# The guard in a float64 weight decode: from ScalarE and VectorE to VectorE and GpSimd

## The chip, the core and the metric

The kernel runs on one NeuronCore of a Trainium2 chip. The core has five engines that each take their own instructions strictly in order: TensorE (PE, with its weight loads shown apart as PEld), VectorE (DVE), ScalarE (ACT), GpSimd (POOL) and SyncE (SP), which here only issues DMAs. The metric is the device time of one execution in microseconds, lower is better. Before the change three runs gave 763.26, 766.6 and 768.91 us, with a median of 766.6 us.

## The reference, cut to what matters

Attention over hash buckets, followed by a gated feed-forward with a short convolution, for 4 batches of 768 rows and 8 heads of 64:

```
q_bucket, k_bucket = 6 sign bits of q @ proj, k @ proj
scores = 0.125 * q @ k.T, masked to -1e9 where the buckets differ
attn   = exp(scores - max) / (sum + 1e-9);  x = attn @ v, heads side by side
h      = relu(x @ w_in)                       # 512 -> 1024
conv   = 3-tap convolution of h along the sequence, weights conv_w
out    = (h * sigmoid(conv)) @ w_out          # 1024 -> 512
```

The inputs `w_in`, `conv_w` and `w_out` are float64. The chip computes in 32 bits, so the kernel reads each weight as two 32-bit words and rebuilds it as a sum of two float32 parts before TensorE uses it. That decode is where the change lies.

## The kernel before, in words

**Attention.** The 32 heads are handled as 16 pairs, and each pair in 12 units of 128 query rows for one head, 192 units in all. A unit multiplies queries with keys into PSUM (`products`, line 250), VectorE copies the scores to SBUF and takes their row maximum (`maximum`, line 260, with a small scaling at line 262), ScalarE takes the exponential (line 265), TensorE transposes the result (line 280), ScalarE copies that back (line 287), and after each four units TensorE multiplies with the values (line 306, 24 matmuls in a row, preceded by two transposes at line 301). VectorE scales that result (`x`, line 315) and GpSimd splits it (lines 316 and 317). VectorE also forms the reciprocal sums (lines 270 and 271) that GpSimd spreads into `rec` (line 274). So four units make one round, about 10 to 11 us long in this part of the program.

**The next pair.** While one pair runs, GpSimd splits the next pair's queries and keys, in tile `R`, into two parts (`hi` at line 168, the rest at line 173), VectorE takes the hash bits (line 186) from a TensorE product (line 183), and SyncE copies the parts to their places (lines 171, 175 and 192). Only when all that has read `R` can the following pair be loaded into it (line 155).

**The weights.** There are 16 blocks of 128 rows by 512 columns, 8 of `w_in` (tiles `wui`, `wli`, `rawi`) and 8 of `w_out` (`wuo`, `wlo`, `rawo`), and one small block of 24 columns for the convolution. One block is decoded per round, from about 30 us to about 212 us in the profile. A block passes through these instructions: the absolute value of the high word on ScalarE (line 86); on VectorE the compare-and-multiply that zeroes small weights (line 88), the shift (line 90), the merge (line 92), the mask (line 94) and the low product (line 96); on ScalarE the rounding (line 104); on GpSimd a subtraction (line 106) and an addition (line 108).

**The order.** All order is written out by hand. The decode is a Python generator, and `background` (line 128) moves every open block one step on per unit: it runs a generator until it yields a number that is at least `stop`, which is 1 during the attention units. So `yield 0` keeps two instructions in the same unit, and `yield 1` or `yield 2` puts the next instruction into the next unit. Blocks that were opened earlier are moved on first. Each engine then executes what stands in its own queue from first to last.

Of the kernel before, what the change touches and what calls it, by code (L numbers as in the profile page):

```python
# [9 lines left out]
I32 = mybir.dt.int32  # L10
U32 = mybir.dt.uint32
AF = mybir.ActivationFunctionType
ALU = mybir.AluOpType
# [12 lines left out]
SCALE = 0.125  # L26
BIG = float(2 ** 33)
MASKED = -8.0e9
F64_MIN = 2.0 ** -15 * 1.125
LAG, EB = 3, 5  # L30
DEFER = 2
FLAG = 3
# [10 lines left out]
def lsh_attention_conv_ffn(ctx, tc, qk, v, hw, w_in, conv_w, w_out, consts, ident_in, out):  # L43
    nc = tc.nc
# [7 lines left out]
    def ring(pool, bufs, shape, dtype, tag, name):  # L52

        k = turns[tag] = (turns.get(tag, -1) + 1) % bufs
        return pool.tile(shape, dtype, tag=f"{tag}{k}", name=name, bufs=1)
# [17 lines left out]
    def decode(raw, n, name):  # L73

        pr = raw.rearrange("p (n two) -> p n two", two=2)  # L80
        lo, hi = pr[:, :, 0].bitcast(U32), pr[:, :, 1].bitcast(F32)
        up, low = (ring(wp, bufs, [P, WC], I32, f"w{x}", f"w{x}{name}")[:, :n]
                   for x, bufs in (("u", 3), ("l", 3)))
        upf, lowf = up.bitcast(F32), low.bitcast(F32)
        V = nc.vector
        nc.scalar.activation(lowf, hi, AF.Abs)
        yield 2
        V.scalar_tensor_tensor(upf, lowf, F64_MIN, hi, ALU.is_ge, ALU.mult)
        yield 1
        V.tensor_scalar(low, up, 3, 0x3FFFFFFF, ALU.logical_shift_left, ALU.bitwise_and)  # L90
        yield 0
        V.scalar_tensor_tensor(up, up, -0x40000000, low, ALU.bitwise_and, ALU.bitwise_or)  # L92
        yield 2
        V.tensor_scalar(low, up, -0x800000, None, ALU.bitwise_and)
        yield 0
        V.scalar_tensor_tensor(lowf, lo, 2.0 ** -52, lowf, ALU.mult, ALU.mult)  # L96
        return upf, lowf

    def split_weight(raw, name):

        up, low = yield from decode(raw, WC, name)
        yield 2
        blk = weights[name] = cp.tile([P, 2, WC], F32R, tag=f"w{name}", name=f"w{name}")
        nc.scalar.copy(blk[:, 0, :], up)
        yield 2
        nc.gpsimd.tensor_tensor(up, up, blk[:, 0, :].bitcast(F32), ALU.subtract)
        yield 1
        nc.gpsimd.tensor_tensor(blk[:, 1, :], up, low, ALU.add)

    def decode_taps(raw):  # L110
        up, low = yield from decode(raw, NFC * 3, "cw")
        nc.vector.tensor_tensor(cw.rearrange("p f k -> p (f k)"), up, low, ALU.add)
# [419 lines left out]
```

## Time and profile before

| | |
|---|---|
| median of 3 runs | 766.6 us (763.26 to 768.91) |
| the profiled execution | 764.44 us, of which its span is 761.6 us |
| PE busy | 722.1 us, 95% of the span |
| ACT busy | 511.9 us, 67% |
| DVE busy | 486.1 us, 64% |
| POOL busy | 294.9 us, 39% |
| mean granted TensorE clock | 0.992 of full speed |

Busy time says how long an engine was executing, not whether anything waited for it. What sets the end is read from the chain of waits, which follows each instruction back to whatever released it. [...] The 2.84 us between the span and the execution's time lie outside the instructions.

### The profile page before, as it was taken

Reading aid. Unit: us, or ns where it says so; the run is one execution under the profiler, and the core shown is the slowest. Engines: PE = TensorE matmul, PEld = TensorE weight load, DVE = VectorE, ACT = ScalarE, POOL = GpSimd, SP = SyncE. Lnnn points to the kernel's source line nnn. Section 1 sums busy time; section 2 is a strip of 40 time slices with the busy share of each in tenths; the row PEclk is TensorE's granted clock in tenths of the full one; section 3 lists DMA queues with packets and bytes.
Section 4 is the critical chain, followed back from the end, with each engine's and each line's share of the span. In section 5 each row is a group of like instructions: output and inputs, shape, how many; then the busy total and the mean of one; then the engine's idle time right before and its main releaser. Section 6 shows DMA issues by size and latency. Waiting matters only on the chain.

```text
span 761.6 us, 12950 instructions
## 1 busy us (share of the span) xinstructions
PE 722.1 (95%) x4648; PEld 595.3 (78%) x4648; DVE 486.1 (64%) x1032; ACT 511.9 (67%) x954; POOL 294.9 (39%) x325
## 2 busy tenths in 40 slices
PE   5989989888889999999999999999999999999997
PEld 3867767665679987777889988777778998778986
DVE  7789978777857555555546655555546665554663
ACT  5877768777755558777765557777775556775554
POOL 4355765566536221433424421333424421113222
PEclk8999999999999999999999999999999999999999
DMA  4666576484422111445632202256361211000011
GB/s 138 157 181 191 128 195 165 117 230 108 116 50 65 60 42 64 118 123 150 140 105 53 73 1 105 48 147 154 95 174 40 63 42 62 2 1 1 0 43 41
DMA packets 30351, 72.13 MB, mean 95 GB/s; under 512 B 5936, under 2 KB 7504, under 8 KB 30288
## 3 DMA queue, kind: packets, MB, share of 16 engines
q1 hardware_dynamic: 30000, 71.27, 34.7%
q8 instruction: 36, 0.59, 0.3%
q14 instruction: 27, 0.22, 0.1%
q10 hardware_dynamic: 288, 0.05, 0.0%
HBM read 27.40 MB, written 6.29 MB: 44 GB/s over the span
## 4 chain that ended last, share of the span: by engine, by line
PE 69%; DVE 18%; DMA 5%; ACT 3%; issue 2%; POOL 1%; SPq 1%; DVEq 0%; POOLq 0%; ACTq 0%
PE o L365 18%; PE h L335 17%; PE v L306 14%; PE t L280 10%; DVE e L260 9%; PE s L250 9%; DMA R<-in_qk 2%; ACT at L287 2%; DMA k<-R 2%; DVE x L315 1%; PE hash L183 1%; PE v L301 1%; DVE wuo L92 1%; DVE wlo L96 1%; DVE st L262 1%
## 5 line engine op out<-in xcount | busy, mean ns | idle before, releaser
L260 DVE TENSOR_SCALAR_CACHE_REDUCE e<-s 128x768 f32<-128x768 f32 x192 | 182.9, 953 | 108.2 <-PE s L250 100.4
L265 ACT ACTIVATE e<-e,st 128x768 f32<-128x768 f32 x192 | 180.8, 941 | 30.0 <-DVE st L262 22.2
L287 ACT COPY at<-t 128x768 f32<-128x768 f32 x192 | 151.8, 792 | 61.1 <-PE t L280 61.1
L280 PE MATMUL t<-ident,e 128*128 128x128 f32 x1152 | 161.5, 277 | 17.4 <-DVE e L260 15.2
L280 PEld LDWEIGHTS t<-ident,e 128*128 128x128 f32 x1152 | 133.0, 141 | 40.1 <-DVE e L260 33.5
L344 DVE SCALAR_TENSOR_TENSOR ht<-ht,cw 128x384 f32<-128x384 f32 (+1 forms) x128 | 113.9, 890 | 71.1 <-ACT ht L342 67.4
L365 PE MATMUL o<-wo,g 128*128 128x512 f32 x576 | 143.0, 394 | 1.0 <-POOL g L354 1.0
L335 PE MATMUL h<-xh,wi 128*128 128x386 f32 x512 | 142.2, 341 | 1.0 <-ACT ht L340 1.0
L306 PE MATMUL v<-at,v 128*64 128x256 f32 x1152 | 137.0, 383 | 0.0
L354 POOL TENSOR_TENSOR g<-ht,g 128x384 fp32r<-128x384 f32 x64 | 72.0, 1124 | 151.9 <-ACT g L353 120.1
L365 PEld LDWEIGHTS o<-wo,g 128*128 128x128 f32 x576 | 107.3, 188 | 21.9 <-POOL g L354 1.4
L250 PE MATMUL s<-K,Q 128*128 128x384 f32 x384 | 117.5, 387 | 3.7 <-DVE e L260 2.7
L274 POOL TENSOR_SCALAR rec<-sums 128x256 f32<-128x256 f32 x48 | 19.5, 406 | 246.7 <-ACT at L287 146.7
L306 PEld LDWEIGHTS v<-at,v 128*64 128x64 f32 x1152 | 82.0, 137 | 41.2 <-issue 7.9
L250 PE MATMUL s<-k,q 96*128 96x384 f32 x384 | 99.8, 341 | 2.3 <-DVE e L260 2.2
L335 PEld LDWEIGHTS h<-xh,wi 128*128 128x128 f32 x512 | 94.1, 188 | 5.0 <-ACT ht L340 1.5
L347 ACT ACTIVATE ht<-ht 128x384 f32<-128x384 f32 x64 | 33.6, 526 | 90.4 <-DVE ht L344 90.2
L335 PE MATMUL h<-xl,wi 128*128 128x386 f32 x256 | 86.8, 339 | 0.0
L250 PEld LDWEIGHTS s<-K,Q 128*128 128x128 f32 x384 | 58.9, 192 | 34.5 <-issue 19.0
L250 PEld LDWEIGHTS s<-k,q 96*128 96x128 f32 x384 | 71.1, 192 | 3.1 <-ACT q L230 3.1
L348 DVE TENSOR_TENSOR ht<-ht 128x384 f32<-128x384 f32 x64 | 43.4, 679 | 33.7 <-ACT ht L347 33.4
L173 POOL TENSOR_TENSOR R<-R,hi 128x768 fp32r<-128x768 f32 x30 | 58.9, 1964 | 0.7
(70 smaller groups left out, 632.9 us busy)
## 6 DMA issues: line engine op xcount, KB each, us to landing
R<-in_qk SPq DMA_DIRECT2D x15, 768.0 KB
K<-hi SPq DMA_DIRECT2D x60, 192.0 KB
v<-in_v SPq DMA_DIRECT2D x16, 384.0 KB
out<-osb SPq DMA_DIRECT2D x24, 256.0 KB
Q<-hi SPq DMA_DIRECT2D x30, 192.0 KB
q<-hi SPq DMA_DIRECT2D x30, 192.0 KB
Q<-R SPq DMA_DIRECT2D x30, 192.0 KB
k<-R SPq DMA_DIRECT2D x30, 192.0 KB
```

Of the source, the lines that this page charges most:

```text
L173: nc.gpsimd.tensor_tensor(lo, R, hi.bitcast(F32), ALU.subtract)
L250: nc.tensor.matmul(self.sp[:, half, :HS], A[:, h, qs], C[:, h, half * HS:(half + 1) * HS], start=(kk == 0), stop=(kk == 1))
L260: nc.vector.tensor_scalar(self.e.rearrange("p (a b) -> p a b", a=2), self.sp[:, :, :HS], MASKED, None, ALU.max, ALU.max, accum_out=self.st ...
L265: nc.scalar.activation(self.e, self.e, AF.Exp, bias=self.st[:, 1:2], scale=SCALE, accum_out=self.sums[:, self.tq, self.h:self.h + 1])
L280: nc.tensor.transpose(self.tp[:, c // 3, c % 3 * P:(c % 3 + 1) * P], self.e[:, c * P:(c + 1) * P], ident)
L287: nc.scalar.copy(pr.at[self.h][:, :, :, self.tq * P:(self.tq + 1) * P], self.tp[:, :, :3 * P].rearrange("p j (c q) -> p j c q", c=3))
L306: nc.tensor.matmul(av[h * D:(h + 1) * D, :QB], vt[:, c, h, :], ats[h][:, c // 3, c % 3, :], start=(c == 0), stop=(c == NCK - 1), tile_posi ...
L335: nc.tensor.matmul(hp[:, :HW], w, x[:, c0:c0 + HW], start=(n == 0), stop=(n == 3 * NCC - 1))
L344: nc.vector.scalar_tensor_tensor(t[:, a:z], ht[:, o + k - 1 + a:o + k - 1 + z], cw[:, f, k:k + 1], t[:, a:z], ALU.mult, ALU.add)
L348: nc.vector.tensor_tensor(t, ht[:, o:o + HS], t, ALU.mult)
L354: nc.gpsimd.tensor_tensor(g[:, 1, :], t, g[:, 0, :].bitcast(F32), ALU.subtract)
L365: nc.tensor.matmul(op, l, r, start=(f == 0 and n == 0), stop=(f == NFC - 1 and n == 2))
```

## The change

The guard no longer zeroes small weights. It clears the sign of the high word on VectorE with an integer AND (line 87 of the changed kernel), and GpSimd then clamps that word, read as a float32, between 2^-15 and the largest finite float32, in place (line 89). The shift (now line 91) works in place on the clamped word, and the merge (now line 93) takes sign and top exponent bit from the raw high word, not from a guarded copy. The mask and the low product stay as they are, at lines 95 and 97; every line from there on has a number higher by one.

```diff
-F64_MIN = 2.0 ** -15 * 1.125
+F32_MAX = 2.0 ** 127 * (2.0 - 2.0 ** -23)
+F64_MIN = 2.0 ** -15
...
-        nc.scalar.activation(lowf, hi, AF.Abs)
+        V.tensor_scalar(low, hi.bitcast(I32), 0x7FFFFFFF, None, ALU.bitwise_and)
+        yield 1
+        nc.gpsimd.tensor_scalar(lowf, lowf, F32_MAX, F64_MIN, ALU.min, ALU.max)
         yield 2
-        V.scalar_tensor_tensor(upf, lowf, F64_MIN, hi, ALU.is_ge, ALU.mult)
-        yield 1
-        V.tensor_scalar(low, up, 3, 0x3FFFFFFF, ALU.logical_shift_left, ALU.bitwise_and)
+        V.tensor_scalar(low, low, 3, 0x3FFFFFFF, ALU.logical_shift_left, ALU.bitwise_and)
         yield 0
-        V.scalar_tensor_tensor(up, up, -0x40000000, low, ALU.bitwise_and, ALU.bitwise_or)
+        V.scalar_tensor_tensor(up, hi.bitcast(I32), -0x40000000, low, ALU.bitwise_and, ALU.bitwise_or)
```

Per block, ScalarE issues one instruction less, VectorE as many as before, and GpSimd one more. Neither SyncE's nor TensorE's order changes. On VectorE the AND stands one unit earlier than the compare-and-multiply stood. The place shown is the round in which the sixth block of `w_in`, `wli_1_1018`, is guarded (in the profile before, 85 us to 93 us). VectorE before, from `x` to the merge:

```order
L315 TENSOR_TENSOR x_1_2_1005<-v_1_2_919,rs_1_2_920 128x256 [waits Activation_49,Pool_49]
L260 TENSOR_SCALAR e_2_2_1_1026,st_2_2_1_1025<-s_2_2_1_1020 128x768 [waits PE_49]
L262 TENSOR_SCALAR st_2_2_1_1025<-st_2_2_1_1025 128x1 [waits DVE_49]
L88 SCALAR_TENSOR_TENSOR wui_1_1017<-wli_1_1018,rawi_1_779 128x512 [waits DMAHW1_49,Activation_49]
L260 TENSOR_SCALAR e_2_3_1_1052,st_2_3_1_1051<-s_2_3_1_1046 128x768 [waits PE_49]
L262 TENSOR_SCALAR st_2_3_1_1051<-st_2_3_1_1051 128x1 [waits DVE_49]
L90 TENSOR_SCALAR wli_1_1018<-wui_1_1017 128x512
L92 SCALAR_TENSOR_TENSOR wui_1_1017<-wui_1_1017,wli_1_1018 128x512 [waits DVE_49]
```

The same stretch of VectorE with the change:

```order
L316 TENSOR_TENSOR x_1_2_1005<-v_1_2_919,rs_1_2_920 128x256 [waits Activation_49]
L87 TENSOR_SCALAR wli_1_1018<-rawi_1_779 128x512 [waits DMAHW1_49]
L261 TENSOR_SCALAR e_2_2_1_1026,st_2_2_1_1025<-s_2_2_1_1020 128x768 [waits PE_49]
L263 TENSOR_SCALAR st_2_2_1_1025<-st_2_2_1_1025 128x1 [waits DVE_49]
L261 TENSOR_SCALAR e_2_3_1_1052,st_2_3_1_1051<-s_2_3_1_1046 128x768 [waits PE_49]
L263 TENSOR_SCALAR st_2_3_1_1051<-st_2_3_1_1051 128x1 [waits DVE_49]
L91 TENSOR_SCALAR wli_1_1018<-wli_1_1018 128x512 [waits Pool_49]
L93 SCALAR_TENSOR_TENSOR wui_1_1017<-rawi_1_779,wli_1_1018 128x512 [waits DVE_49]
```

The AND stands ahead of the two row maxima, nothing stands between them, and the shift, which waited for no other engine, now waits for GpSimd. GpSimd in the same round, with the change (`hi` and `R` belong to the next pair, `wui_1_885` and `wli_1_886` to the block before):

```order
L318 TENSOR_TENSOR xl_1_659<-x_1_2_1005,xh_1_658 128x256 [waits Pool_49]
L169 TENSOR_SCALAR hi_3_1_1009<-R_3_724 128x768 [waits DMAHW4_49,DMAHW5_49,DMAHW3_49,DMAHW2_49]
L107 TENSOR_TENSOR wui_1_885<-wui_1_885,wi_1_1015 128x512 [waits Activation_49]
L89 TENSOR_SCALAR wli_1_1018<-wli_1_1018 128x512 [waits DVE_49]
L174 TENSOR_TENSOR R_3_724<-R_3_724,hi_3_1_1009 128x768 [waits Pool_49]
L109 TENSOR_TENSOR wi_1_1015<-wui_1_885,wli_1_886 128x512 [waits Pool_49]
```

The clamp, `L89`, is the one new row. It stands behind the subtraction of the previous block and ahead of two instructions that read two tensors each; before, those followed the subtraction at once.

## Rows read from the trace of the kernel before

**Rows 1.** The page: span, and busy time of each engine.
```profile
span 761.6 us, 12950 instructions
PE 722.1 (95%) x4648; PEld 595.3 (78%) x4648; DVE 486.1 (64%) x1032; ACT 511.9 (67%) x954; POOL 294.9 (39%) x325
```

**Rows 2.** Stretches: bounds, length, busy per engine (instructions), clock, DMA share, GB/s.
```profile
20.00:120.00 100.00, 90.11 (x644) 71.77 (x641) 84.43 (x193) 75.25 (x137) 55.01 (x57) 0.98 0.63 166
120.00:212.00 92.00, 78.70 (x576) 60.61 (x576) 74.31 (x167) 67.94 (x124) 55.59 (x57) 1.00 0.58 151
212.00:762.00 550.00, 541.25 (x3382) 455.89 (x3378) 311.93 (x650) 356.68 (x676) 176.10 (x201) 1.00 0.26 71
```

**Rows 3.** The chain that ended last, 20 to 215 us: start, length, what.
```profile
45.62 1.13 DVE wui L88
...
64.70 0.41 DVE x L315
...
79.91 2.21 DVE wui L92
...
102.52 4.26 DMA R<-in_qk
...
124.30 2.20 DVE wuo L92
...
199.90 0.58 ACT wlo L86
```

**Rows 4.** Line 88: ns min/median/max, first and last start; then its waits.
```profile
L88 DVE SCALAR_TENSOR_TENSOR wui<-wli,rawi x8: 692/1185/2286, 33.2 to 110.5; 128x512 f32<-128x512 f32 x8
L88 DVE SCALAR_TENSOR_TENSOR wuo<-wlo,rawo x8: 1168/1424/1761, 121.7 to 200.5; 128x512 f32<-128x512 f32 x8
...
  ACT wlo L86: 9.3, 8
```

**Rows 5.** Timeline of GpSimd, 85 to 94 us: start, length, instruction.
```profile
85.80 0.41 POOL L274 TENSOR_SCALAR rec<-sums 128x256 f32<-128x256 f32 x1 [2.55 <-DVE sums L271]
...
87.37 0.82 POOL L168 TENSOR_SCALAR hi<-R 128x768 fp32r<-128x768 f32 x1
88.16 1.71 POOL L106 TENSOR_TENSOR wui<-wui,wi 128x512 f32<-128x512 f32 x1
89.82 2.03 POOL L173 TENSOR_TENSOR R<-R,hi 128x768 fp32r<-128x768 f32 x1
91.81 1.73 POOL L108 TENSOR_TENSOR wi<-wui,wli 128x512 fp32r<-128x512 f32 x1
```

**Rows 6.** Timeline of VectorE, the merge at 59 us, then 85 to 93 us.
```profile
59.07 1.64 DVE L92 SCALAR_TENSOR_TENSOR wui<-wui,wli 128x512 int32<-128x512 int32 x1
...
85.53 0.41 DVE L315 TENSOR_TENSOR x<-v,rs 128x256 f32<-128x256 f32 x1
...
87.58 1.15 DVE L88 SCALAR_TENSOR_TENSOR wui<-wli,rawi 128x512 f32<-128x512 f32 x1 [0.58 <-ACT wli L86]
...
89.71 0.45 DVE L90 TENSOR_SCALAR wli<-wui 128x512 int32<-128x512 int32 x1
90.19 2.21 DVE L92 SCALAR_TENSOR_TENSOR wui<-wui,wli 128x512 int32<-128x512 int32 x1
```

**Rows 7.** Lines 96, 106 and 173: ns min/median/max, first and last start.
```profile
L96 DVE SCALAR_TENSOR_TENSOR wli<-rawi,wli x8: 691/693/702, 39.2 to 117.7; 128x512 f32<-128x512 uint32 x8
...
L106 POOL TENSOR_TENSOR wui<-wui,wi x8: 1267/1280/1729, 44.9 to 122.2; 128x512 f32<-128x512 f32 x8
...
L173 POOL TENSOR_TENSOR R<-R,hi x30: 1827/1846/2359, 23.2 to 599.5; 128x768 fp32r<-128x768 f32 x30
```

**Rows 8.** Timeline of TensorE at 107 us: the hash after the load of R.
```profile
106.92 0.85 PE L183 MATMUL hash<-R,hw_sb 128*32 128x384 f32 x8 [2.61 <-DMA R<-in_qk]
```

**Rows 9.** Timelines of GpSimd and VectorE in a round of `w_out`, 157 to 160 us.
```profile
157.54 1.61 POOL L108 TENSOR_TENSOR wo<-wuo,wlo 128x512 fp32r<-128x512 f32 x1
...
159.71 0.42 DVE L90 TENSOR_SCALAR wlo<-wuo 128x512 int32<-128x512 int32 x1
```

## The prediction
> **What bounds the kernel now.** I read the page first, then the stretches, then the chain of waits, then the timelines of VectorE and GpSimd side by side. TensorE is busy for 722.1 of 761.6 us [rows 1], but not evenly. From 212 us on it is busy for 541.25 of 550 us; from 20 to 212 us, where the weights are decoded, for 168.8 of 192 us, while VectorE is busy for 158.7 [rows 2]. So the change can only act on this stretch, where TensorE and VectorE take turns on the chain. A delay in it moves all that follows. The chain shows which decode instructions matter: in the rounds of `w_in` the merge (2.21 us at 80 us) and once the compare-and-multiply (1.13 us at 45 us) [rows 3].
>
> The number to look at is 2.21. The merge takes 0.69 us when nothing disturbs it, as its twin in shape, the low product, shows [rows 7]. In the round at 85 us it started at 90.19, GpSimd's split of `R` had started at 89.82 and ended at 91.85, and the merge ended at 92.40, 0.55 us later [rows 5, 6]. The shift in the same round ended at 90.16, 0.29 us after the subtraction that ended at 89.87. So a VectorE instruction that is issued behind a GpSimd one is held to its end, and then finishes 0.29 us (one tensor) or 0.55 us (two tensors) later. That is the mechanism on which my sum rests. [...]
>
> **What is removed.** Sixteen absolute values go from ScalarE. They bound VectorE only while it waited for them, 9.3 us in the eight rounds of `w_out` [rows 4]. Those eight compare-and-multiplies (median 1.42 us) and that wait, though, stand where VectorE has nothing else before TensorE delivers new scores, after its 24 value matmuls; so I cost them at nothing. One absolute value, at 200 us, is itself on the chain, with 0.58 us [rows 3]: -0.58. In `w_in`'s rounds the compare-and-multiply is on the path at 45 us; new scores come soon after, so between 0 and 1.13 I take half: -0.55. Elsewhere its going is counted inside the rounds below.
>
> **What is added on VectorE.** The AND has a strided input. Its price lies between 0.42, the shift of equal shape [rows 9], and 0.69, the strided low product [rows 7]. In the rounds of `w_in` it comes right behind `x`, just when GpSimd runs `rec`. In the round at 85 us it could start at 85.86, `rec` ends at 86.21 [rows 5], so it would end at 86.50 and its successor start at 86.44: 0.58 late, whichever end of its price holds. There `x`, a row maximum and then TensorE's transposes follow each other on the chain, as at 65 us [rows 3]; two such rounds besides the one at 96 us: 3 x 0.58 = +1.7. In `w_out`'s rounds it stands one row maximum later, in VectorE's slack: 0.
>
> **What is added on GpSimd.** The clamp's price is not in the trace. One-tensor instructions there take 0.41 us for 256 columns and 0.82 for 768 [rows 5], so 512 columns make 0.61. Bounds: 0.41, and 1.28 for the subtraction, which reads two tensors [rows 7]. I take 0.61, since the clamp reads one.
>
> **The new wait.** Now the round at 85 us. VectorE loses 1.15 for the compare-and-multiply and 0.58 of waiting [rows 6] and gains 0.58 for the AND, so the shift is ready at 89.71 - 1.15 = 88.56. GpSimd: the AND pushes its work by 0.25, so `hi` ends at 88.19 + 0.25 = 88.44; the subtraction, no longer held, takes 1.28 to 89.72; the clamp ends at 90.34. The shift has to wait 1.8 us for it. GpSimd goes straight on (the split started 0.05 before the subtraction's recorded end [rows 5]), whereas VectorE still has to see the signal. So the split goes first, 1.83 us [rows 7] to 92.17. The shift ends 0.29 later, at 92.46. It has let go of the memory just as GpSimd's addition takes it, 1.28 us to about 93.7, and the merge, which needs the shift, ends 0.55 behind that, at 94.25 instead of 92.40: **+1.85**. What is queued behind it on VectorE is the row maximum of the next unit, and TensorE waits for that.
>
> The same queue (clamp, then two instructions of two tensors) stands in four of `w_in`'s and `w_out`'s first rounds where the merge is on the chain: those with the merges at 59, 80, 90 and 124 us [rows 3, 6], 4 x 1.85 = +7.4. In the rounds at 35, 70, 101 and 114 us VectorE waits for TensorE's scores right behind the merge, and the delay fits in there: 0. In `w_out`'s later rounds GpSimd is through its work before the shift comes up. The tightest is the one at 157 us: the addition ends at 159.15, or 158.9 without its hold, plus 0.61 makes 159.5, and the shift comes at 159.71 [rows 9]: 0, with 0.2 us to spare.
>
> One thing gives time back. At 106.9 us TensorE waits 2.61 us for the load of `R` [rows 3, 8]. That load starts later only by what happened before its copies were queued, about 3 us, so lateness from 77 to 104 us eats into the wait: -2.6.
>
> **The sum:** 7.4 + 1.7 - 2.6 - 0.55 - 0.58 = +5.4. Against the profiled execution (764.44 us, which is span plus 2.84) that is 769.8; it lies 2.2 below the median of the runs, 766.6, against which I predict: **772.0**. A difference below 1%, 7.7 us, can't be told from no change in measuring this kernel, so this forecast is no change.
>
> **The rivals.**
>
> *Held once.* The shift gets in between clamp and split. Then only the merge is held, and each of the four rounds costs 0.4 + 1.83 + 0.55 behind the clamp's 90.34, that is 93.15 and +0.75. Three of these, two or three ANDs and the credits leave about +1.3 at 107 us, then 0.75 - 0.58: +1.5, **768.1**. For it: a gap of only 0.05 us. Against it: GpSimd's instructions of that round follow each other without any gap [rows 5].
>
> *A gain.* The clamp is done before the shift comes, nothing is held, and the compare-and-multiplies are simply gone. Then the round at 124 us gives 1.15 plus the merge's hold of 1.51 less the AND's 0.58, about 2.1; the rounds at 80 and 90 us mostly vanish into the wait for `R`; with 0.55 + 0.58 and less two ANDs it is about -2, at most -4: **763.6**. Against it: the shift comes at 88.56, when GpSimd has two instructions to go.
>
> *A dear clamp.* This one ends slower. If the clamp costs 1.28, each of the four rounds is later by 0.67 more (+2.7), and the spare 0.2 us in `w_out` is gone: 0.3 us in about half of eight rounds (+1.2). The sum is 5.4 + 3.9 = +9.3, **775.9**, slower by 1.2%; it decides from a clamp of about 0.85 on. For it: no row shows a minimum or maximum on GpSimd. Against it: three kinds of one-tensor work there fit one line. [...]
>
> *The change moves nothing:* all lateness disappears in waits for TensorE and for `R`. Then it is 766.6; it is inside the range already.
>
> **How the numbers follow.** The forecast has 0.50, held once and nothing moved 0.22 together, a gain 0.08, a dear clamp 0.20. The range runs from the gain's time, 763, to 779, which takes in the dear clamp up to 1.5 us; under 0.2 is left out. Slower by over 1% takes three quarters of the dear clamp (0.15) and a sixth of the forecast (0.09), faster by over 1% would need nearly four times the gain: 0.03.
>
> **What would show it.** In the profile after: about sixteen clamps of 0.6 us; the shift held behind the split and ending 0.29 after it, in the rounds at 59, 80, 90 and 124 us; VectorE's wait for GpSimd, some 1 to 2 us in each; merges of over 1.5 us behind the addition; next to no wait for `R` at 107 us; and everything from 212 us on as before, only later. A clamp over 0.85 us, or a shift of 0.42 us right behind the clamp, would make the forecast wrong.

## The result, and the profile after the change

The changed kernel takes 771.03 us, the kernel before 764.61 us beside it (medians of 20 runs each), 6.4 us more. The ratio of the runs is 1.0076, with a 95% interval of 1.0062 to 1.0089, which makes 5.8 us. The twenty runs put the kernel before 2.0 us lower than the three runs from which the prediction started (766.6 us). One of the twenty runs of the changed kernel, the profiled one, took 2464.9 us, with its groups of matmuls on average 2.5 to 2.8 times as long; the ratio leaves it out, and the profile after is that of a further run of the same kernel (769.93 us, label e1_again below). In the lines below, L107 is the subtraction, L109 the addition and L174 the split of `R`.

The page of after, in the columns of [rows 1]:

```profile
span 768.1 us, 12929 instructions
PE 720.4 (94%) x4648; PEld 590.8 (77%) x4648; DVE 478.0 (62%) x1032; ACT 503.2 (66%) x937; POOL 299.8 (39%) x342
```

VectorE has less to do than before (478.0 instead of 486.1 us), ScalarE too (503.2 instead of 511.9), GpSimd hardly more, and yet the time grew. To compare equal work, take the stretch from 20 us to the same `x` near its end, at 216.72 us before and at 223.75 us after. It grew from 196.7 to 203.8 us, while TensorE's busy time in it went from 172.5 to 170.9 us and VectorE's from 159.9 to 152.0: the time went into waiting. From there to the end both kernels take about the same (544.9 us before, 544.4 after). The span is 6.5 us longer, the profiled execution 5.5 (769.93 against 764.44). The next two fences show one round on VectorE and on GpSimd, the same one as in [rows 5, 6] (the round whose merge stood at 90 us):

```profile
88.84 0.39 DVE L316 TENSOR_TENSOR x<-v,rs 128x256 f32<-128x256 f32 x1
89.15 0.64 DVE L87 TENSOR_SCALAR wli<-rawi 128x512 int32<-128x512 int32 x1
89.72 0.94 DVE L261 TENSOR_SCALAR_CACHE_REDUCE e<-s 128x768 f32<-128x768 f32 x1
...
93.63 2.05 DVE L91 TENSOR_SCALAR wli<-wli 128x512 int32<-128x512 int32 x1 [1.72 <-POOL wli L89]
95.71 1.66 DVE L93 SCALAR_TENSOR_TENSOR wui<-rawi,wli 128x512 int32<-128x512 int32 x1
97.29 0.94 DVE L261 TENSOR_SCALAR_CACHE_REDUCE e<-s 128x768 f32<-128x768 f32 x1
```

```profile
89.11 0.41 POOL L275 TENSOR_SCALAR rec<-sums 128x256 f32<-128x256 f32 x1 [4.22 <-DVE sums L272]
...
90.83 0.84 POOL L169 TENSOR_SCALAR hi<-R 128x768 fp32r<-128x768 f32 x1
91.63 1.28 POOL L107 TENSOR_TENSOR wui<-wui,wi 128x512 f32<-128x512 f32 x1
92.99 0.61 POOL L89 TENSOR_SCALAR wli<-wli 128x512 f32<-128x512 f32 x1
93.56 1.83 POOL L174 TENSOR_TENSOR R<-R,hi 128x768 fp32r<-128x768 f32 x1
95.34 1.48 POOL L109 TENSOR_TENSOR wi<-wui,wli 128x512 fp32r<-128x512 f32 x1
```

Read across. VectorE is through its row maxima at 91.91 us and waits 1.72 us for the clamp, which ends at 93.60. By then the split is already running (from 93.56); the shift, issued at 93.63, ends at 95.68, which is 0.29 after the split's end at 95.39. The addition has taken over at 95.34, and the merge ends at 97.37, 0.55 after the addition's end at 96.82. From `x` to the end of the merge the round takes 8.53 us; before it took 6.87 (85.53 to 92.40 [rows 6]). The AND takes 0.64, of which a part is hold: it ends 0.27 after `rec`; where GpSimd runs nothing beside it (at 171.67 and 205.30 us) it takes 0.42. Which instructions are held is read from this trace: shift and AND, one tensor each, and the merge, with two. The row maximum is not: it takes 0.94 us from 89.72, while GpSimd runs `xh` and `xl` (89.48 to 90.87), and 0.94 from 97.29, after GpSimd's last instruction of the round. So the prediction's "a VectorE instruction" is too wide.

The lines of the clamp and the shift, all instances: minimum, median and maximum in ns, first and last start, and then the waits for the clamp.

```profile
L89 POOL TENSOR_SCALAR wli<-wli x8: 612/613/617, 35.5 to 115.5; 128x512 f32<-128x512 f32 x8
L89 POOL TENSOR_SCALAR wlo<-wlo x8: 612/613/615, 127.4 to 208.4; 128x512 f32<-128x512 f32 x8
...
  DVE wli L91: 10.4, 7
  DVE wlo L91: 1.7, 1
```

```profile
L91 DVE TENSOR_SCALAR wli<-wli x8: 417/1524/2048, 36.1 to 116.2; 128x512 int32<-128x512 int32 x8
L91 DVE TENSOR_SCALAR wlo<-wlo x8: 416/419/2047, 128.1 to 211.1; 128x512 int32<-128x512 int32 x8
```

All sixteen clamps take 0.61 us. VectorE waits 12.1 us for them, in eight rounds and no others. In one of these nothing stands behind the clamp in GpSimd's queue, and the shift takes 0.43 us (at 36.11). In the other seven it is issued 0.07 us after GpSimd's next instruction has started, and takes 1.48 to 2.05. In five of the seven the merge is then held too (1.65 to 2.22 us); in the other two, at 70 and 105 us, it is not (0.69). In `w_out`'s seven later rounds the shift finds the clamp done; it takes 0.42 us in five of them, 0.48 and 0.72 in the others.

### The profile page after: what moved, and what is told of

It is laid out like the page before. It is cut to its first block, busy times and chain, and to the rows that moved or that the text cites. A ratio compares the mean times of both kernels' runs of the same rounds, so it can differ in the third digit from the quotient of the medians.

```text
span 2462.9 us, 12929 instructions
## 1 busy us (share of the span) xinstructions
PE 2454.5 (100%) x4648; PEld 1383.3 (56%) x4648; DVE 469.1 (19%) x1032; ACT 515.1 (21%) x937; POOL 293.9 (12%) x342
## 4 chain that ended last, share of the span: by engine, by line
PE 100%; DMA 0%; DVE 0%; issue 0%
PE t L281 19%; PE s L251 19%; PE h L336 19%; PE v L307 19%; PE o L366 19%; PE hash L184 2%; PE v L302 1%; PE hash L212 0%; DMA hw_sb<-in_hw 0%; DVE osb L372 0%
## 5 line engine op out<-in xcount | busy, mean ns | idle before, releaser
L281 PE MATMUL t<-ident,e 128*128 128x128 f32 x1152 | 528.3, 696 | 0.0
L366 PE MATMUL o<-wo,g 128*128 128x512 f32 x576 | 491.3, 1104 | 0.0
L307 PE MATMUL v<-at,v 128*64 128x256 f32 x1152 | 476.9, 1087 | 0.0
L281 PEld LDWEIGHTS t<-ident,e 128*128 128x128 f32 x1152 | 307.0, 267 | 210.4 <-issue 123.6
L336 PE MATMUL h<-xh,wi 128*128 128x386 f32 x512 | 402.9, 891 | 0.0
L366 PEld LDWEIGHTS o<-wo,g 128*128 128x128 f32 x576 | 249.1, 433 | 200.9 <-issue 200.6
L251 PE MATMUL s<-K,Q 128*128 128x384 f32 x384 | 318.2, 962 | 0.0
L336 PEld LDWEIGHTS h<-xh,wi 128*128 128x128 f32 x512 | 218.6, 427 | 117.8 <-issue 98.0
L251 PE MATMUL s<-k,q 96*128 96x384 f32 x384 | 284.0, 874 | 0.0
L336 PE MATMUL h<-xl,wi 128*128 128x386 f32 x256 | 231.7, 905 | 0.0
L251 PEld LDWEIGHTS s<-k,q 96*128 96x128 f32 x384 | 170.9, 446 | 52.2 <-issue 34.1
```

Source lines behind the costliest of these rows:

```text
L251: nc.tensor.matmul(self.sp[:, half, :HS], A[:, h, qs], C[:, h, half * HS:(half + 1) * HS], start=(kk == 0), stop=(kk == 1))
L281: nc.tensor.transpose(self.tp[:, c // 3, c % 3 * P:(c % 3 + 1) * P], self.e[:, c * P:(c + 1) * P], ident)
L307: nc.tensor.matmul(av[h * D:(h + 1) * D, :QB], vt[:, c, h, :], ats[h][:, c // 3, c % 3, :], start=(c == 0), stop=(c == NCK - 1), tile_posi ...
L336: nc.tensor.matmul(hp[:, :HW], w, x[:, c0:c0 + HW], start=(n == 0), stop=(n == 3 * NCC - 1))
L366: nc.tensor.matmul(op, l, r, start=(f == 0 and n == 0), stop=(f == NFC - 1 and n == 2))
```

## The experiments

All were run five rounds each beside the kernel before on the same chip: e1, e2, e4 and e6 on one (before 765.25 us there), e3, e5, e9 and e10 on another (before 764.05). Times are medians, ratios are to before on the same chip, and the 95% interval stands in brackets. A kernel of one chip is compared with a kernel of the other by their differences to before.

**e1_again: the changed kernel, unedited.**

> The changed kernel again, unedited, for a profile of an ordinary execution. Theory (the shift waits for the clamp, is then held behind GpSimd's split or addition, and the merge behind the next): some +5.4 us over before, with the shift ending 0.29 us after the split and the merge 0.55 us after the addition in the rounds at about 59, 80, 90 and 124 us, and clamps of about 0.61 us. Rival (held once): the shift takes 0.42 us right behind the clamp and each of these rounds is later by only 0.75. Rival (a dear clamp): clamps above 0.85 us, and waits in the rounds of w_out too.

770.87 us, ratio 1.0072 (1.0045 to 1.0098). This is the result again, with the profile shown above.

**e4_no_clamp: the AND stays, the clamp is left out** (so sizes are not limited).

```diff
         yield 1
-        nc.gpsimd.tensor_scalar(lowf, lowf, F32_MAX, F64_MIN, ALU.min, ALU.max)
         yield 2
```

> The clamp is left out (part of the guard's computation), the AND and the two free units stay, so the shift waits for no other engine. Theory: the shift is held behind the subtraction and the merge behind the split, as before the change: 0 in the four rounds, two ANDs +1.2, -0.55 and -0.58: within 0.5 us of before, about 764.6. Rival (AND is the cost): +3 to +5 over before, near the change. Rival (compare-and-multiply was on the path in every round): 5 us or more faster than before.

761.13 us, ratio 0.9958 (0.9931 to 0.9986). By the medians the change without its clamp gains 4.1 us on before; with it, it loses 5.6. So the clamp, 0.61 us of GpSimd in sixteen places, costs 9.7 us (8.7 by the ratios), and the rest of the change is a gain. That is a miss of the expectation, which had this kernel within 0.5 us of before; the result lies nearer to the last rival named there. The round that corresponds to the one above, on VectorE:

```profile
91.98 1.36 DVE L90 TENSOR_SCALAR wli<-wli 128x512 int32<-128x512 int32 x1
93.37 2.20 DVE L92 SCALAR_TENSOR_TENSOR wui<-rawi,wli 128x512 int32<-128x512 int32 x1
```

The shift (L90 here) comes up without a wait and is held behind the subtraction; the merge (L92) is held behind the split, like the 2.21 us of before [rows 6]. So the merge's hold is still there, and a hold of the shift that is 0.7 us shorter, but the 1.7 us of waiting are not. Where each of the 4.1 us comes from this kernel's profile can't tell: its profiled execution took 768.9 us, with TensorE's clock at a lower level in three places (mean 0.57 of full speed from 44 to 52 us, 0.62 from 108 to 116, 0.60 from 192 to 196; below).

**e6_clamp_twice: the clamp done twice in a row.**

```diff
         nc.gpsimd.tensor_scalar(lowf, lowf, F32_MAX, F64_MIN, ALU.min, ALU.max)
+        nc.gpsimd.tensor_scalar(lowf, lowf, F32_MAX, F64_MIN, ALU.min, ALU.max)
         yield 2
```

> The clamp runs twice in a row, one more GpSimd instruction of 128x512 per block. Theory: each of the four rounds is later by another 0.61 us (three of them before the load of R, where the wait is used up already), +2.4, and the spare 0.2 us of the w_out rounds is gone, +1 to +2: 3.5 to 4.5 us over the change, about 775. Rival (a single wait, with slack behind it): under 1 us. Rival (GpSimd's total load is the bound): 17 x 0.61, 10 us.

777.12 us, ratio 1.0149 (1.0116 to 1.0183): 6.2 us over the change, more than the 3.5 to 4.5 expected. GpSimd, with the clamps L89 and L90, and VectorE, with the shift L92:

```profile
96.54 0.61 POOL L89 TENSOR_SCALAR wli<-wli 128x512 f32<-128x512 f32 x1
97.23 0.61 POOL L90 TENSOR_SCALAR wli<-wli 128x512 f32<-128x512 f32 x1
97.81 1.84 POOL L175 TENSOR_TENSOR R<-R,hi 128x768 fp32r<-128x768 f32 x1
```

```profile
97.88 2.06 DVE L92 TENSOR_SCALAR wli<-wli 128x512 int32<-128x512 int32 x1 [2.22 <-POOL wli L90]
```

The second clamp starts 0.69 us after the first, and the same picture follows it. Taken from one `x` to the next, five rounds grew by 0.67 to 0.70 us each (the one above from 11.93 to 12.62): the clamp's price goes into the time one to one where the shift waits for it and the merge is held. That is 3.4 us; the expectation had four such rounds and 2.4 us. Two more rounds grew by 2.3 and 1.9 us, with a lower TensorE clock in each (0.72 of full speed from 44 to 48 us, 0.50 from 104 to 108); how much of that the second clamp makes was not separated. In `w_out`'s later rounds the spare time is used up too: those at a full clock (1.00) are 0.2 to 0.3 us longer than before. With two clamps, 1.30 us together, the kernel is slower than before by 1.5%; the third rival had 1.2% for a clamp of 1.28.

**e2_clamp_early: the clamp one unit earlier, ahead of the subtraction in the program.**

```diff
         V.tensor_scalar(low, hi.bitcast(I32), 0x7FFFFFFF, None, ALU.bitwise_and)
-        yield 1
+        yield 0
         nc.gpsimd.tensor_scalar(lowf, lowf, F32_MAX, F64_MIN, ALU.min, ALU.max)
+        yield 1
         yield 2
```

> The clamp is issued in the same unit as the AND, one unit earlier, so that it stands ahead of the subtraction in GpSimd's queue; the same instructions otherwise. Theory: the shift finds the clamp done, or nearly, and the merge is held only behind the subtraction; worked from the round at 85 us it ends at 91.2 instead of 94.3 (before: 92.4). Sum against before: -0.55 - 0.58 + 1.2 for two ANDs, about -1.2 in the round at 124 us, the rest lost in the wait for R: about -1.4, so 763 and some 7 us faster than the change. Rival (the clamp's work on GpSimd is what costs, wherever it stands): the same as the change, +5 to +6. Rival (the AND on VectorE's path is what costs): still +1.7 and more over before.

766.47 us, ratio 1.0019 (0.9994 to 1.0043): 4.4 us less than the change, no measurable difference to before. The direction is as expected, the size is not: some 7 us were forecast. GpSimd does the same work as in the change, so that work alone does not make the loss; where it stands in the queue does. GpSimd, and VectorE with the shift L92 and the merge L94, show why the gain is not larger:

```profile
92.44 0.83 POOL L170 TENSOR_SCALAR hi<-R 128x768 fp32r<-128x768 f32 x1
93.35 0.61 POOL L89 TENSOR_SCALAR wli<-wli 128x512 f32<-128x512 f32 x1
93.93 1.28 POOL L108 TENSOR_TENSOR wui<-wui,wi 128x512 f32<-128x512 f32 x1
```

```profile
94.00 1.49 DVE L92 TENSOR_SCALAR wli<-wli 128x512 int32<-128x512 int32 x1 [0.48 <-POOL wli L89]
95.52 2.22 DVE L94 SCALAR_TENSOR_TENSOR wui<-rawi,wli 128x512 int32<-128x512 int32 x1
```

I had overlooked that `hi` (L170) still stands ahead of the clamp. The wait shrinks to 0.48 us, but the shift still comes just after GpSimd's next instruction and is held 1.1 us behind the subtraction. "Earlier" was not early enough.

**e3_clamp_vector: the clamp on VectorE, at the same place.**

```diff
-        nc.gpsimd.tensor_scalar(lowf, lowf, F32_MAX, F64_MIN, ALU.min, ALU.max)
+        V.tensor_scalar(lowf, lowf, F32_MAX, F64_MIN, ALU.min, ALU.max)
```

> The clamp runs on VectorE instead of GpSimd, in the same unit (between the two row maxima), all else as in the change. Theory (what costs is the shift's wait for GpSimd and the place it then gets behind split and addition): the rounds fall back to those of the kernel before, x to x about 10.3 us instead of 11.9 in the change, some 4 to 6 us faster than the change although VectorE has 17 instructions more; 764 to 767. Rival (VectorE's work is the bound): slower than the change by up to 16 x 0.42, 7 us.

762.22 us, ratio 0.9975 (0.9956 to 0.9995): the whole guard is computed, and the kernel is 1.8 us faster than before, where the change is 5.6 us slower than before on its chip. So moving the clamp gave back 7.4 us, more than the 4 to 6 expected. The same round on VectorE:

```profile
86.65 0.42 DVE L89 TENSOR_SCALAR wli<-wli 128x512 f32<-128x512 f32 x1
86.98 0.95 DVE L261 TENSOR_SCALAR_CACHE_REDUCE e<-s 128x768 f32<-128x768 f32 x1
...
88.05 1.24 DVE L91 TENSOR_SCALAR wli<-wli 128x512 int32<-128x512 int32 x1
89.32 2.21 DVE L93 SCALAR_TENSOR_TENSOR wui<-rawi,wli 128x512 int32<-128x512 int32 x1
```

The clamp costs VectorE 0.42 us and the row maximum behind it starts 0.33 after it; VectorE waits for no other engine here, and the merge's hold is that of before. VectorE is busy for 87.59 us from 20 to 120 us, 8 more than in the change (with 203 instructions in that stretch instead of 181), and the end comes earlier.

**e9_both_later: as e3, but AND and clamp one unit later, in one place.**

```diff
-        V.tensor_scalar(low, hi.bitcast(I32), 0x7FFFFFFF, None, ALU.bitwise_and)
         yield 1
-        nc.gpsimd.tensor_scalar(lowf, lowf, F32_MAX, F64_MIN, ALU.min, ALU.max)
+        V.tensor_scalar(low, hi.bitcast(I32), 0x7FFFFFFF, None, ALU.bitwise_and)
+        yield 0
+        V.tensor_scalar(lowf, lowf, F32_MAX, F64_MIN, ALU.min, ALU.max)
```

> AND and clamp both on VectorE, both between the two row maxima, where the compare-and-multiply stood; the first row maximum comes right behind x again. Theory: against the kernel with the clamp alone on VectorE this saves the AND's 0.58 us in the rounds where x, row maximum and transposes are the chain: 1 to 2 us faster than that one, within 2 us of before. Rival (the AND's place does not matter): the same as that one.

762.74 us, ratio 0.9997 (0.9976 to 1.0017). The AND is out of the way of the first row maximum (`x` at 85.71, row maximum at 86.04), but the clamp is now held itself, 0.94 instead of 0.42 us. The 1 to 2 us expected over e3 did not come: no gain can be told.

**e5_before_idle: the kernel before, with one idle instruction of GpSimd where the clamp would stand**, on a tile of its own that nobody waits for.

```diff
+    idle = cp.tile([P, 128], F32, name="idle")
+    nc.gpsimd.memset(idle, 1.0)
...
+        nc.gpsimd.tensor_scalar(idle, idle, 4.0, 0.5, ALU.min, ALU.max)
```

> The kernel before with one GpSimd instruction more per block, a minimum and maximum over 128 columns of an own tile, at the clamp's place in GpSimd's queue; nothing waits for it. Theory of holds: in the rounds at 80, 90 and 124 us the merge is now held behind this 0.3 us instruction instead of the 1.83 us split, so it takes about 0.8 us instead of 2.2; the time is 0 to 3 us better than before, with more work on GpSimd. Rival (GpSimd's load or its queue is the bound): 17 x 0.3 us, up to 5 us slower than before.

766.1 us, ratio 1.0027 (1.0009 to 1.0046): a miss, slightly slower, not faster. VectorE (merge L95, mask L97), then GpSimd:

```profile
92.11 0.69 DVE L95 SCALAR_TENSOR_TENSOR wui<-wui,wli 128x512 int32<-128x512 int32 x1
...
95.02 1.02 DVE L97 TENSOR_SCALAR wli<-wui 128x512 int32<-128x512 int32 x1
```

```profile
91.88 0.35 POOL L90 TENSOR_SCALAR idle<-idle 128x128 f32<-128x128 f32 x1
92.31 2.19 POOL L176 TENSOR_TENSOR R<-R,hi 128x768 fp32r<-128x768 f32 x1
94.47 1.29 POOL L111 TENSOR_TENSOR wi<-wui,wli 128x512 fp32r<-128x512 f32 x1
```

The merge is indeed unheld, 0.69 instead of 2.21 us. The row maximum behind it now waits for TensorE's scores and comes only 0.31 us earlier after `x` than in before (6.48 against 6.79). But GpSimd's next two instructions are later, and the next VectorE instruction, the mask, is held in the merge's stead: 1.02 instead of 0.42. The rounds are longer by 0.3 us each (10.57 against 10.29). So an extra GpSimd instruction by itself, though a shorter one, makes about 2 us. The wait for the clamp is not in this kernel; that it makes most of the rest is argued, since no run has the wait without the holds behind it.

**e10_merge_later: the kernel before, shift and merge one unit later** in `w_in`'s rounds and `w_out`'s first, clear of GpSimd's two long instructions.

```diff
+        late = name.startswith("i") or name == "o0"
...
+        if late:
+            yield 1
...
-        yield 2
+        yield 0 if late else 2
```

> The kernel before, with shift and merge of the eight w_in blocks and the first w_out block moved one unit later, next to mask and low product; same instructions. Theory: there GpSimd is through with split and addition, so the merge takes 0.69 us instead of up to 2.21; the rounds at 46, 80, 90 and 124 us get shorter by up to 1.5 us each, part of it lost in the wait for R at 107 us: 2 to 4 us faster than before, about 762. Rival (merges were held in time that TensorE's scores would have taken anyway): no change.

769.83 us, ratio 1.0078 (1.0051 to 1.0106): a clear miss. VectorE, first the row maximum of before that follows the merge of [rows 6], then this kernel (shift L93, merge L95, mask L97, low product L99):

```profile
92.32 0.94 DVE L260 TENSOR_SCALAR_CACHE_REDUCE e<-s 128x768 f32<-128x768 f32 x1
```

```profile
90.01 0.41 DVE L318 TENSOR_TENSOR x<-v,rs 128x256 f32<-128x256 f32 x1
...
96.50 0.96 DVE L263 TENSOR_SCALAR_CACHE_REDUCE e<-s 128x768 f32<-128x768 f32 x1 [2.23 <-PE s L253]
...
97.57 0.42 DVE L93 TENSOR_SCALAR wli<-wui 128x512 int32<-128x512 int32 x1
98.02 0.69 DVE L95 SCALAR_TENSOR_TENSOR wui<-wui,wli 128x512 int32<-128x512 int32 x1
98.75 0.43 DVE L97 TENSOR_SCALAR wli<-wui 128x512 int32<-128x512 int32 x1
99.21 0.69 DVE L99 SCALAR_TENSOR_TENSOR wli<-rawi,wli 128x512 f32<-128x512 uint32 x1
99.82 0.95 DVE L263 TENSOR_SCALAR_CACHE_REDUCE e<-s 128x768 f32<-128x768 f32 x1
```

Shift, merge, mask and low product are held no more, and the round takes 11.16 us instead of 10.29. The four stand in a row ahead of one row maximum, so that shift and merge put it off by 1.18 us (97.57 to 98.75). What was saved is small: the row maximum behind the value matmuls, which waits for TensorE now (96.50), comes 6.49 us after `x` (90.01); with the held merge ahead of it, in before, it came 6.79 after `x`, since the 24 value matmuls and the scores behind them run beside the hold. So a hold of 1.5 us cost 0.3 there, as in e5, and the move lost 1.18 to gain it. Refuted is that moving the two instructions here would gain.

## Why the prediction was right

**The forecast**, +5.4 us, no change by the bound of 1%: measured +5.6 in e1_again, and in the result +5.8 by the ratio and +6.4 by the medians. That the time itself is within 1 us (772.0, measured 771.03) is luck in part, since the forecast started from a median of before that lay 2.0 us too high. The prediction also said that a difference below 1% can't be told from none; with the runs of the result it can, since the interval lies wholly above 1. The mechanism came as described: the wait of 1.72 us for the clamp (forecast 1.8), the split going first, the shift ending 0.29 after it, the merge 0.55 after the addition. That it is the memory that VectorE is held by ("let go of the memory" in the prediction's sum) no run shows; they show these times. In the round with the merge at 59 us the addition went ahead of the split, and the same two holds came in the other order (shift 1.48, merge 2.22 us). e4 and e3 show that the clamp's place on GpSimd is the cause, since without it, or with it on VectorE, the loss is gone; e2 shows that it is mainly its place in the queue, since the work on GpSimd stays the same there; e6 shows that its price passes through. How the loss divides between the wait and the two holds is read from the traces alone.

**The clamp's price**, interpolated to 0.61: 0.613. The third rival is out. (Its bound of about 0.85 us was low: by the prediction's own terms that price makes some +6.5 us, under the 7.7 of 1%.)

**The first two rivals.** Held once: in none of the seven rounds where an instruction stood behind the clamp did the shift get in between the two. A gain: as a whole only with the clamp removed or moved to VectorE, but in the change itself in one round, which the prediction did not count. In before a merge of 2.21 us stood on the chain at 48.77 us too; in after the clamp of that round was done at 47.42, the shift came at 47.46 and took 0.42, and the merge took 0.87.

**Term by term.** The forecast's terms stand beside differences of the time from one `x` to the next, e1_again less before:

| round that begins in before at | forecast | measured |
| --- | --- | --- |
| 54, 75, 86, 120 us: held shift and merge | 4 x 1.85 = +7.4 | 1.64 + 1.54 + 1.64 + 1.63 = +6.45 |
| AND ahead of a row maximum | 3 x 0.58 = +1.7 | 65 us: +0.15; 96 us: +0.16; 31 us: +0.44 |
| 41 us: compare-and-multiply gone | -0.55 | -0.58 |
| 106 us: wait for `R` gone | -2.6 | -1.45 |
| 196 us: absolute value gone | -0.58 | +0.13 |
| 151 us (`w_out`) | 0 | +1.56 |

Without the last row the measured ones make +5.3. The sum was near because errors cancelled. They also cancel between the clamp and the rest: by e4 all but the clamp makes -4.1 us, where the prediction's terms (as the expectation of e4 adds them) come to about 0, and the clamp makes 9.7. So what went was worth more than the terms for it, and the clamp cost more; in which rounds, e4's profile can't show.

- *The compare-and-multiply at 41 us* came out by luck. Its term was half of 1.13, a guess. What went there is more, the compare-and-multiply and most of the holds of shift and merge, and VectorE now waits 2.12 us for TensorE's scores at 50.90; when these come sets the 0.58.

- *The AND* was mis-sized. In the round at 65 us the next row maximum does start 0.56 later. But the 24 value matmuls (before, then after) take 2.81 us instead of 3.20, which gives 0.39 back:

```profile
67.06 3.20 PE L306 MATMUL v<-at,v 128*64 128x256 f32 x24
```

```profile
69.22 2.81 PE L307 MATMUL v<-at,v 128*64 128x256 f32 x24
```

  It fits that the absolute value, whose going I had costed at nothing there, stood on ScalarE (66.03 to 66.72) ahead of the copies that these matmuls read, and that the second of these copies now ends 0.49 earlier after `x`. The other kernels fit too: 3.17 to 3.20 us occurs in the three that keep the absolute value (before, e5, e10) and in none of the others. In the round at 54 us the AND makes nothing beyond the held merge.

- *The wait for `R`* is gone, as forecast: the hash follows the matmuls ahead of it without a wait, where [rows 8] had 2.61 us. TensorE and VectorE of after:

```profile
109.33 0.85 PE L184 MATMUL hash<-R,hw_sb 128*32 128x384 f32 x8
...
120.83 0.88 PE L281 MATMUL t<-ident,e 128*128 128x128 f32 x6 [1.59 <-DVE e L261]
```

```profile
116.17 2.04 DVE L91 TENSOR_SCALAR wli<-wli 128x512 int32<-128x512 int32 x1 [1.82 <-POOL wli L89]
118.24 1.66 DVE L93 SCALAR_TENSOR_TENSOR wui<-rawi,wli 128x512 int32<-128x512 int32 x1
```

  From `x` to the next row maximum the round gains 2.35 us. But from there to the row maximum behind the merge it loses 0.92: this is the round with the merge at 114 us, for which I had put 0 since VectorE waited for TensorE there. The same queue forms, and now TensorE waits 1.59 us for VectorE. A slack that was read in before did not outlast the change. The row holds one thing more: in before's profile TensorE runs at the lower clock, 0.50 of full speed, from 107.7 to 111 us in this round (last section), in after's it does not, and this pair of profiles can't say how much of the 2.35 that is.

- *The absolute value at 200 us* stood on the chain, and its going brought nothing in that round. The chain led from it to ScalarE's copy of `rs` at 202.04 us, but TensorE's value matmuls, which that copy needs too, ended at 201.97: only 0.07 us could be gained. In after the copy waits 0.52 us for them. The chain names what came last, not by how much.

- *The round at 151 us* has nothing of the change in it that is late; it is told below.

**`w_out`'s later rounds**: 0, as forecast, but for the one at 151 us. Five of the seven shifts take 0.42 us there, as in [rows 9], right after the row maximum.

## What to carry to other kernels

Work that is handed from VectorE to GpSimd and back can cost more than its own duration (here 9.7 us for sixteen clamps of 0.61). In this kernel GpSimd went straight on to its next instruction and VectorE's came 0.07 us behind it, seven times of seven, so VectorE waited for the step and then was held behind what followed it. Count the step's successors in GpSimd's queue, and compare with doing the step where its result is used, even if that engine looks the busier one (here 0.42 us on VectorE; moving it there gave back 7.4 us, with VectorE waiting in eight of sixteen handovers). And a hold is worth what TensorE does not cover (here 0.3 of 1.5 us, in e5 and e10): before removing one, look where its time would go.

## What the runs showed that I had not expected

TensorE's granted clock falls to a lower level (0.50 of full speed in before from 107.7 to 111 us, 0.50 in e6 from 104 to 108 and in e4 from 112 to 116), by an estimate from the mean clock of each stretch for some 3 to 7 us at a time, in each of the nine profiles compared here, and not in the same places. Many of the falls follow a wait of TensorE for `R`, at 43 to 45 us (e2, e4, e5, e6, e9) or at 105 to 109 us (before, e3, e5), others stand elsewhere. In before it is the stretch after the wait of 2.61 us [rows 8]; bounds, length, busy times per engine, clock, DMA share, GB/s:

```profile
104.00:112.00 8.00, 5.39 (x31) 4.43 (x30) 5.34 (x12) 4.86 (x9) 5.73 (x7) 0.79 0.72 221
```

In e1_again it is not there, but in the round that was 1.56 us too long. The stretch, then TensorE:

```profile
156.00:164.00 8.00, 6.46 (x40) 4.71 (x42) 4.74 (x15) 4.90 (x10) 7.03 (x8) 0.79 0.61 156
```

```profile
159.13 1.54 PE L281 MATMUL t<-ident,e 128*128 128x128 f32 x6 [1.44 <-DVE e L261]
...
161.02 3.50 PE L307 MATMUL v<-at,v 128*64 128x256 f32 x24
```

Six transposes take 1.54 us instead of 0.88, and the value matmuls 3.50 instead of 2.81, after a wait of 1.44 us. A wait of 1.59 us at 120.83 had no such effect (0.88), nor had the 2.36 us for `R` at 44.61. In e9 the clock fell at a wait of 1.73 us (at 43.8 us) and not at one of 2.44 us (at 106.5). So the length of the wait before it does not sort them, and what decides it stays open. e4's execution of 768.9 us has three such stretches, while nine of that kernel's other eleven took 759.6 to 762.4 us; e6's has seven. Some cost nothing, others up to some 4 us (the round at 41 us takes 16.6 us in e4, with such a stretch, and 12.3 in e3, without), so that one profile against another can't tell terms of this size, and the medians of many runs have to.
